# A fifth block product by seven small ones, in a written-out order, in the channel stage of routing attention and an MLP mixer

## The chip, the cores and the metric

The kernel runs on one core of one Trainium2 chip. The metric is the device time of one execution in microseconds (us). All data are float32.

## The reference

Four batches of 768 tokens with 8 heads of 64 go through attention in which a query sees only the keys of its own cluster, and the result, 768 x 512 for each batch, goes through an MLP mixer: a token stage, and a channel stage with 1536 hidden channels.

```python
q_assign = np.argmax(np.einsum('bhsd,hcd->bhsc', q_n, c_n), axis=-1)
k_assign = np.argmax(np.einsum('bhsd,hcd->bhsc', k_n, c_n), axis=-1)
mask = q_assign[:, :, :, None] == k_assign[:, :, None, :]
scores = np.where(mask, scale * np.matmul(q, k.transpose(0, 1, 3, 2)), -1e9)
...                                            # softmax, times v; x is (4, 768, 512)
h = np.maximum(x.transpose(0, 2, 1) @ w_tok1, 0.0) @ w_tok2
u = x + h.transpose(0, 2, 1)
h2 = np.maximum(u @ w_ch1, 0.0) @ w_ch2        # w_ch1 512 x 1536, w_ch2 1536 x 512
return u + h2
```

## The kernel before

The kernel goes through three stages: attention (16 pairs of heads), the token stage (batches 0 and 1, then 2 and 3), and the channel stage, a batch at a time in the order 0, 2, 3, 1. The change lies in the channel stage and the hand-over to it. The order of issue is written out by hand: each engine runs its instructions in the order in which the Python code issues them, and semaphores make an instruction wait for data and for a buffer that is still read.

**A batch and its parts.** The channel stage takes a batch's hidden channels in three parts. A part has a first layer (`ch1_pair`, line 784), which makes hidden blocks, and a second layer (`ch2_chunks`, line 960), which multiplies them by the second weights and adds the result to x. Both layers are written as a 2 x 2 block product with seven products in place of eight (Winograd's form). The seven are in the table `SEVEN` (line 551):

| name | left x right | | name | left x right |
|---|---|---|---|---|
| p1 | A11·B11 | | c12 | S4·B22 |
| p5 | S1·T1 | | c22 | S3·T3 |
| c11 | A12·B21 | | c21 | A22·T4 |
| u2 | S2·T2 | | | |

The S are sums of left blocks (weights in the first layer) and the T are sums of right blocks (the batch's transposed tokens `uT`); `winograd_left` and `winograd_right` yield their four steps each as one VectorE instruction.

**Products of small ones.** In the first part of the first batch (`ch1_plain`) the first layer runs its seven products in two chunks each, and a chunk is 2 matmuls with 384 columns that add up (12 chunks go through `big`, the last two, of c21, come late). In the other 11 parts (`ch1_sets`, line 864) four of the seven are themselves split into 2 x 2 blocks and done by seven small products with 192 columns, with sums of sums: they are called Y (c11), P (p5), Z (c12) and X (c21). `set_lefts` and `set_rights` (lines 602 and 620) name their blocks; `set_left_sums(part)` makes the weights' sums once, in the first batch; `set_right_sums` makes the right sums anew for each batch, into the tile `uTss`. The other three products, p1, u2 and c22, stay big: 2 chunks each, written `big`.

A small product goes to a bank of PSUM (8 banks; tags X, Z with three each and Y with two) and is then added to a block in SBUF by VectorE, at line 566 (`add`), or copied by ScalarE. A second product that accumulates in a bank waits until the first one's addition has read it. In the code, `direct` writes both halves of a bank, `chain` adds up p1, u2, c22 and c21 in one bank with an addition after each, and `column` adds p5 to two blocks.

**What fills the gaps.** `others` is a list of steps on VectorE (sums of weights and operands); `late` is a list with the end of the first layer. `between`, called after each big product of the first layer and after each of the 21 products of the second (`by_turns`, line 746), issues the next of both. `u_steps` turn the next batch's tokens (ScalarE copies and DMA transposes); three of them, `beside`, are issued in the first layer of the batch's last part. `u_sums` yields T1 to T4 of the next batch.

**At a batch's end.** T1 and two sums of P are issued within the last products; then come two sums of Y and Z together and T2, and the rest go to `others`:

```python
yz, x, p = steps
yz[0]()
yz[1]()
next(usums)
others += [lambda: next(usums)] * 2
others.append(lambda: [step() for step in (yz[2], p[2], yz[3], p[3])])
others += [lambda: None, lambda: (x[0](), x[1]()), lambda: (x[2](), x[3]())]
```

Batch 1 is spilled to DRAM after the first half of the token stage and comes back into x0's place when batch 0 is written. Three numbers that say whether this fast path held are counted in the first batch (`fits`, `fits_count`) and read by every engine with `values_load` (`fits_load`, line 1004) ahead of the last second layer; a branch at the end uses them.

Of the kernel before, what the change touches and what calls it, by code (L numbers as in the profile page):

```python
# [50 lines left out]
def kernel(  # L51
# [49 lines left out]
    tokpool = pool("tokpool", 1, tokens)  # L101
    staging = fast.enter_context(ExitStack())
# [30 lines left out]
    spill = spilled.tile([P, NJ, DM], F32, name="spill")  # L133
    xs = [(x1pool if b == 1 else xpool).tile([P, NJ, DM], F32, name=f"x{b}") for b in range(B)]
# [466 lines left out]

    def set_lefts():
        if "l2" not in pools:
            pools["l2"] = pools["w2sums"].tile([P, 4, 3, HS], F32, name="w1ss")
        l2 = pools["l2"]
        yx = W["ch1"].rearrange("p f (i r c) -> p f i r c", i=2, r=2)[:, 2:4]
        pz = pools["w1s"][:, 0:3:2].rearrange("p i f (r c) -> p f i r c", r=2)
        for n, both in enumerate((yx, pz)):
            blocks = [both[:, f, :, r] for r in range(2) for f in range(2)]
            sums_ = [l2[:, 2 * n : 2 * n + 2, m] for m in range(3)]  # L610
            yield dict(
                zip(("A11", "A12", "A21", "A22", "S1", "S2", "S4", "S3"), blocks + sums_ + blocks[2:3])
            )
# [6 lines left out]
    def set_rights():  # L620
        uT, R, r2 = pools["uT"], pools["R"], pools["r2"]
        yz = uT[:, :, 2:4].rearrange("p n f (k t) -> p n f k t", k=2)
        x, p = (R[name].rearrange("p f (k t) -> p f k t", k=2) for name in ("T4", "T1"))
        for blocks, sums_ in (
            ([yz[:, :, f, k] for f in range(2) for k in range(2)], [r2[:, 0:2, m] for m in range(3)]),
            ([x[:, f, k] for f in range(2) for k in range(2)], [r2[:, 2, m] for m in range(3)]),
            ([p[:, f, k] for f in range(2) for k in range(2)], [r2[:, 3, m] for m in range(3)]),
        ):
            yield dict(
                zip(("B11", "B12", "B21", "B22", "T1", "T2", "T4", "T3"), blocks + sums_ + blocks[1:2])  # L630
            )

    def set_right_sums():

        pools["r2"] = pools["w2sums"].tile([P, 4, 3, HS // 2], F32, name="uTss")
        return [list(winograd_right(blocks)) for blocks in set_rights()]

    def set_blocks():

        (yx, pz), (yz, x, p) = (list(y) for y in (set_lefts(), set_rights()))  # L640
        left = {name: {k: a[:, i] for k, a in two.items()} for two, i, name in
                ((yx, 0, "Y"), (yx, 1, "X"), (pz, 0, "P"), (pz, 1, "Z"))}
        right = {"Y": {k: b[:, 0] for k, b in yz.items()}, "Z": {k: b[:, 1] for k, b in yz.items()},
                 "X": x, "P": p}
        return left, right
# [94 lines left out]
    def between(n=1):  # L740
        if late:
            late.pop(0)()
        for _ in range(min(n, len(others))):
            others.pop(0)()

    def by_turns(n, product, of, last=False, after=()):
# [10 lines left out]
        for m in range(len(order) // 2):  # L757
# [9 lines left out]
            between()  # L767
# [16 lines left out]
    def ch1_pair(part, sets, beside):  # L784
# [6 lines left out]
        p5, c12 = (pools["mlp"].tile([P, 2, HS], F32, name=k) for k in ("p5", "c12"))  # L791
# [10 lines left out]

        def big(psum, a, r, i, start):
            product(psum, a, r, i, start)
            between()
            if a != "A11" and beside:
                beside.pop(0)()
# [13 lines left out]
        def sums_34():  # L821
            nc.vector.scalar_tensor_tensor(
                out=h2["S3"], in0=c12, scalar=0.0, in1=a11, op0=ALU.max, op1=ALU.subtract
            )
            sub(h2["S4"], a12, h2["S2"])

        (ch1_sets if sets else ch1_plain)(
            part, product, big, relu, a11, a12, a22, p5, c12, sum_1, sum_2, sums_34
        )

    def ch1_plain(part, product, big, relu, a11, a12, a22, p5, c12, sum_1, sum_2, sums_34):
# [24 lines left out]
        def late_(i):  # L856
            product(X[i], "A22", "T4", i, False)
            nc.scalar.activation(out=a12[:, i], in_=X[i], func=ACT.Relu)
            (sums_34 if i else sum_2)()
# [4 lines left out]
    def ch1_sets(part, product, big, relu, a11, a12, a22, p5, c12, sum_1, sum_2, sums_34):  # L864

        left, right = set_blocks()
        n0, n1 = slice(0, HS // 2), slice(HS // 2, HS)

# [7 lines left out]
        def direct(bank, which, start=True):  # L876
            small(bank[:, n0], which, "c11", start)
            small(bank[:, n1], which, "c12", start)

        def chain(q, which, name, x):  # L880

            small(q[:, n0], which, name, name == "p1")
            src = q[:, n0]
            if len(x.shape) == 3:
                src = src.unsqueeze(1).to_broadcast([P, 2, HS // 2])
            add(x, src, x)

        def column(z, which, x):
            small(z[:, n0], which, "p5")
            add(x[:, :, n1], z[:, n0].unsqueeze(1).to_broadcast([P, 2, HS // 2]), x[:, :, n1])  # L890

        X = [ptile("X", HS), None]
        big(X[0], "A11", "B11", 0, True)
        nc.scalar.copy(out=a11[:, 0], in_=X[0])  # L894
        ybe = ptile("Y", HS)
        direct(ybe, "Y")
        add(a11[:, 0], ybe, a11[:, 0])
        X[1] = ptile("X", HS)
        big(X[1], "A11", "B11", 1, True)
        nc.scalar.copy(out=a11[:, 1], in_=X[1])  # L900
        pbe = ptile("Z", HS)
        direct(pbe, "P")
        nc.scalar.copy(out=p5[:, 0], in_=pbe)
        yq, pq = ptile("Y", HS), ptile("Z", HS)
        chain(yq, "Y", "p1", a11[:, 0, n0])
        chain(pq, "P", "p1", p5[:, 0, n0])
        big(X[0], "S2", "T2", 0, False)
        chain(yq, "Y", "u2", a11[:, 0, n1])
        yz, pz = ptile("X", HS), ptile("Z", HS)
        column(yz, "Y", a11)  # L910
        chain(pq, "P", "u2", p5[:, 0, n1])
        small(pz[:, n0], "P", "p5")
        nc.scalar.copy(out=p5[:, 1, n1], in_=pz[:, n0])
        relu(a11[:, 0])
        add(p5[:, 0, n1], pz[:, n0], p5[:, 0, n1])
        add(c12[:, 0], X[0], p5[:, 0])
        big(X[1], "S2", "T2", 1, False)
        chain(yq, "Y", "c22", a11[:, 1, n1])
        chain(pq, "P", "c22", p5[:, 1, n1])
        direct(ybe, "Z")  # L920
        chain(yq, "Y", "c21", a11[:, 1, n0])
        small(pq[:, n0], "P", "c21", False)
        nc.scalar.copy(out=p5[:, 1, n0], in_=pq[:, n0])
        relu(a11[:, 1])
        add(c12[:, 0], ybe, c12[:, 0])
        chain(yz, "Z", "p1", c12[:, 0, n0])
        add(c12[:, 1], X[1], p5[:, 1])
        big(X[0], "S3", "T3", 0, False)
        add(a22[:, 0], X[0], p5[:, 0])
        relu(a22[:, 0])  # L930
        chain(yz, "Z", "u2", c12[:, 0, n1])
        column(pbe, "Z", c12)
        big(X[1], "S3", "T3", 1, False)
        add(a22[:, 1], X[1], p5[:, 1])
        relu(a22[:, 1])
        chain(yz, "Z", "c22", c12[:, 1, n1])
        direct(X[0], "X", False)
        nc.scalar.copy(out=a12[:, 0], in_=X[0])
        small(X[1][:, n0], "X", "c21", False)
        nc.scalar.copy(out=a12[:, 1], in_=X[1])  # L940
        chain(yz, "Z", "c21", c12[:, 1, n0])
        chain(yq, "X", "p1", a12[:, 0, n0])
        sum_1()

        def late_1():
            chain(yq, "X", "u2", a12[:, 0, n1])
            column(pz, "X", a12)
            sum_2()

        def late_2():  # L950
            chain(yq, "X", "c22", a12[:, 1].rearrange("p (k t) -> p k t", k=2))
            relu(a12)
            sums_34()

        late.extend([late_1, late_2])
# [166 lines left out]
    for b in (0, 2):  # L1122
# [26 lines left out]
        if b == 2:  # L1149
            take(turning, len(turning))  # L1150
            usums = u_sums()
            tok2_chunks(b, {13: lambda: next(usums)})
        else:
# [3 lines left out]
            nc.sync.dma_start(spill, xs[1])  # L1157
# [7 lines left out]
    batches = (0, 2, 3, 1)  # L1165
    for n, b in enumerate(batches):
        turning = []
        for part in range(3):
# [8 lines left out]
            ch1_pair(part, not first, [turning.pop(0) for _ in turning[:UCOLS]])  # L1177
# [5 lines left out]
            if n == 0 and part == 2:  # L1183
                others += set_left_sums(0)
            if last:
                both = fits_load()
            after = {}
# [15 lines left out]
            if part == 2 and not last:  # L1203

                yz, x, p = steps
                yz[0]()
                yz[1]()
                next(usums)

                others += [lambda: next(usums)] * 2  # L1210
                others.append(lambda: [step() for step in (yz[2], p[2], yz[3], p[3])])
                others += [lambda: None, lambda: (x[0](), x[1]()), lambda: (x[2](), x[3]())]
                if n == 0:
                    xs[1] = xpool.tile([P, NJ, DM], F32, name="x0")
                    nc.sync.dma_start(xs[1], spill)
# [182 lines left out]
    with tc.If(both < 3 * P) as fit:  # L1398
# [33 lines left out]
```

## Time and profile before

| | us |
|---|---|
| median of 4 runs (823.25 to 823.74) | 823.34 |
| profiled execution | 823.32 |
| its span | 821.5 |
| TensorE busy | 814.3 |
| VectorE busy | 631.2 |
| ScalarE busy | 374.6 |
| GpSimd busy | 30.6 |

In the profile PE is TensorE, PEld its loading of weights, DVE VectorE, ACT ScalarE, POOL GpSimd and SP the engine that issues most DMAs. Matmuls are shown as pipelined records, so their durations overlap; the distance from one start to the next is the pace. A float32 matmul is two records. Line 798 is the first layer's big product, line 871 the small product, line 966 the second layer's product; lines 563 and 566 are `sub` and `add` on VectorE, line 810 the relu and lines 894 to 940 copies on ScalarE. The channel stage starts at 393.5 us of the span; its parts start at 429.9, 465.4, 500.6, 535.9, 570.9, 605.8, 641.3, 676.2, 711.2, 746.5 and 781.4.

### The profile page before, as it was taken

How to read it: one execution, taken by the hardware profiler on the slowest of the kernel's cores; microseconds unless marked ns; L12 is line 12 of the kernel's file. 1: busy time of each engine (PE TensorE's matmuls, PEld its weight loads, DVE VectorE, ACT ScalarE, POOL GpSimd, SP SyncE). 2: the span in 40 equal slices, each digit the busy share in tenths (PEclk: the TensorE clock that was granted, in tenths of full speed). 3: DMA queues.
4: the chain of work that ended last, by engine and by line, in shares of the span. 5: the costliest groups of instructions: out<-in, count | busy, mean ns of one | idle time of the engine just before them, and what ended most of it. 6: DMA issues, size and time to landing. Idle time of an engine off the chain costs nothing.

```text
span 821.5 us, 11693 instructions
## 1 busy us (share of the span) xinstructions
PE 814.3 (99%) x4348; PEld 535.5 (65%) x4348; DVE 631.2 (77%) x1206; ACT 374.6 (46%) x573; POOL 30.6 (4%) x28
## 2 busy tenths in 40 slices
PE   8999999999999999999999999999999999999997
PEld 4444444444444444444588888888888888888876
DVE  6879898989898978859797788755777566785655
ACT  5588776777878776127202154121441204511120
POOL 1001010111011000000000000000000000000000
PEclk9999999999999999999999999999999999999999
DMA  9797666767676434143000025000140001400002
GB/s 156 132 168 146 134 142 122 149 141 160 131 160 136 98 101 122 51 129 77 0 1 1 4 45 183 1 0 1 38 118 0 1 1 30 125 1 1 1 0 81
DMA packets 184258, 63.41 MB, mean 77 GB/s; under 512 B 172800, under 2 KB 176896, under 8 KB 183936
## 3 DMA queue, kind: packets, MB, share of 16 engines
q1 hardware_dynamic: 182592, 62.18, 34.7%
q8 instruction: 36, 0.59, 0.3%
q10 hardware_dynamic: 1600, 0.39, 0.2%
q14 instruction: 30, 0.25, 0.1%
HBM read 36.21 MB, written 7.86 MB: 54 GB/s over the span
## 4 chain that ended last, share of the span: by engine, by line
PE 98%; DVE 1%; issue 0%; ACT 0%; DVEq 0%; ACTq 0%
PE sc L413 19%; PE av L455 15%; PE pX L966 15%; PE pX L798 12%; PE pZ L966 7%; PE ph L534 5%; PE pY L871 5%; PE pZ L871 4%; PE pX L871 4%; PE pY L966 4%; PE pX L774 3%; PE small L491 2%; PE pZ L774 1%; PE small L304 1%; PE pZ L798 1%; PE pY L774 1%
## 5 line engine op out<-in xcount | busy, mean ns | idle before, releaser
L437 ACT ACTIVATE ex<-sc 128x768 f32<-128x768 f32 x192 | 150.9, 811 | 27.2 <-PE sc L413 15.5
L413 PE MATMUL sc<-qkT 64*128 64x384 f32 x768 | 155.3, 483 | 0.0
L445 DVE TENSOR_TENSOR sum<-sum,ex 128x768 f32<-128x768 f32 x128 | 127.8, 998 | 28.0 <-ACT ex L437 15.8
L455 PE MATMUL av<-ex,va 128*64 128x384 f32 x768 | 127.4, 488 | 0.0
L566 DVE TENSOR_TENSOR x<-pX,x 128x256 f32<-128x256 f32 (+1 forms) x168 | 76.1, 461 | 38.2 <-PE pX L966 37.7
L455 PEld LDWEIGHTS av<-ex,va 128*64 128x64 f32 x768 | 53.7, 137 | 71.7 <-issue 68.0
L413 PEld LDWEIGHTS sc<-qkT 64*128 64x128 f32 x768 | 67.8, 187 | 38.3 <-issue 38.0
L810 ACT ACTIVATE hA<-hA 128x384 f32<-128x384 f32 (+1 forms) x57 | 34.0, 597 | 85.5 <-DVE hA L566 85.5
L566 DVE TENSOR_TENSOR hA<-pY,hA 128x192 f32<-128x192 f32 (+1 forms) x90 | 36.7, 408 | 45.4 <-PE pY L871 42.7
L798 PE MATMUL pX<-uT,wc 128*128 128x384 f32 x192 | 69.8, 487 | 0.0
L894 ACT COPY hA<-pX 128x384 f32<-128x384 f32 x11 | 5.3, 478 | 131.3 <-PE pX L798 131.3
L413 PE MATMUL sc<-ohT 64*128 64x384 bf16 x384 | 62.4, 323 | 0.0
L462 ACT COPY avrows<-av 128x768 uint16<-128x768 uint16 x32 | 25.6, 799 | 43.5 <-PE av L455 43.5
L566 DVE TENSOR_TENSOR x<-pZ,x 128x256 f32<-128x256 f32 (+1 forms) x84 | 36.6, 459 | 11.4 <-PE pZ L966 11.3
L798 PEld LDWEIGHTS pX<-uT,wc 128*128 128x128 f32 x192 | 35.4, 190 | 14.7 <-issue 0.6
L534 PE MATMUL ph<-x,wt 128*128 128x512 f32 x96 | 41.6, 593 | 0.0
L413 PEld LDWEIGHTS <-ohT 64*128 64x128 bf16 x384 | 18.7, 94 | 33.9 <-issue 9.6
L966 PE MATMUL pX<-wc,hA 128*128 128x256 f32 x144 | 36.9, 380 | 0.3 <-ACT hA L940 0.3
L711 ACT COPY uT<-ucols 128x768 uint16<-128x768 uint16 x32 | 33.2, 1051 | 4.8 <-DMA ucols<-urows 4.8
L966 PE MATMUL pZ<-wc,hS 128*128 128x256 f32 x144 | 35.0, 379 | 0.0
L966 PE MATMUL pY<-wc,hA 128*128 128x256 f32 x144 | 35.0, 379 | 0.0
L798 PE MATMUL pX<-uTs,w1s 128*128 128x384 f32 x96 | 34.9, 486 | 0.0
(189 smaller groups left out, 1312.2 us busy)
## 6 DMA issues: line engine op xcount, KB each, us to landing
raw<-in_moe_w_ch_dram SPq DMA_DIRECT2D x24, 512.0 KB, 4.4
va<-in_v_dram SPq DMA_DIRECT2D x16, 384.0 KB, 3.6
out_dram<-x SPq DMA_DIRECT2D x24, 256.0 KB, 2.3
qk<-in_k_dram SPq DMA_DIRECT2D x60, 96.0 KB, 3.8
qk<-in_q_dram SPq DMA_DIRECT2D x60, 96.0 KB, 3.4
raw<-in_moe_w_tok_dram SPq DMA_DIRECT2D x3, 512.0 KB, 4.5
raw<-in_moe_w_tok_dram SPq DMA_DIRECT2D x4, 384.0 KB, 3.8
spill<-x SPq DMA_DIRECT2D x1, 1536.0 KB, 5.1
```

Source lines behind the costliest of these rows:

```text
L413: nc.tensor.matmul(sc[:, h, 0:HS], lhsT=src[rows, 1, j], rhs=src[rows, 0, HJ * qh : HJ * qh + HJ], start=start, stop=not start,)
L437: nc.scalar.activation(out=ex, in_=sc[:, :, 0:HS], func=ACT.Exp, scale=SM_SCALE)
L445: nc.vector.tensor_tensor(out=acc, in0=acc if j > 1 else st["ex", qh, 0], in1=st["ex", qh, j], op=ALU.add)
L455: nc.tensor.matmul(av[h * D : (h + 1) * D], lhsT=st["va"][:, h, j], rhs=ex[:, h], start=(j == 0), stop=(j == NJ - 1),)
L534: nc.tensor.matmul(pf, lhsT=W["tok1"][:, j, t * P : (t + 1) * P], rhs=xs[b][:, j], start=(j == 0), stop=(j == NJ - 1),)
L566: nc.vector.tensor_tensor(out=dst, in0=a, in1=b, op=ALU.add)
L711: nc.scalar.copy(out=out, in_=pools.pop(("ucols", i)).rearrange("p w j t -> p w (j t)"))
L774: nc.tensor.matmul(psum, lhsT=A[a][:, i], rhs=R[r], start=start, stop=True, skip_group_check=not start,)
L798: nc.tensor.matmul(psum, lhsT=A[a][:, k, c], rhs=R[r][:, k], start=start and k == 0, stop=k == 1, skip_group_check=not start,)
L810: nc.scalar.activation(out=x, in_=x, func=ACT.Relu)
L871: nc.tensor.matmul(psum, lhsT=left[which][a][:, part * P : part * P + P], rhs=right[which][r], start=start, stop=True, skip_group_check=no ...
L966: nc.tensor.matmul(psum, lhsT=h2[a][:, k, i * P : (i + 1) * P], rhs=Bw[w][:, part + 3 * k], start=start and k == 0, stop=k == 1, skip_grou ...
```

## The change

S3·T3 (c22) becomes a fifth product done by seven small ones, U. For this there are a block more in `set_lefts` and `set_rights`, a tile `u3` for its result and larger tiles for the sums (5 sets in place of 4). The order of the first layer is written out as a list of names, `CH1`, with a table of banks, `BANKS`. The names read so, with W one of Y, P, Z, X, U: `Wa Wd Wf Wg` are the small products p1, u2, c22 and c21 in one bank, `Wz` is p5, `Wbe` the two direct ones; `+Wa` and so on is the addition on VectorE that reads the bank; `Wc0 Wcz Wcg` are copies on ScalarE. `p1_i` and `u2_i` are the big products' chunks, `a11_i` a copy, `V C B E` additions that put the blocks together, `r11 r22 r12` relus, `s1` to `s4` the second layer's left sums. `yz0` to `u3`, `p2`, `p3`, `T2` to `T4` are the right sums, issued here in the first part of a batch only (`extra`). What stands after the first `|` is issued after the second layer's products, one group each: S1 comes there, after the first product.

The tile of batch 3 gets a place of its own in the token stage and is spilled as well, and both spilled batches come back when two batches before them are written. `between` issues a late step or others, no longer both, and the number of others is chosen so that they last to the end of the second layer; `ch1_sets` issues none. The counts are read after the tenth product of the last second layer.

```diff
-    spill = spilled.tile([P, NJ, DM], F32, name="spill")
-    xs = [(x1pool if b == 1 else xpool).tile([P, NJ, DM], F32, name=f"x{b}") for b in range(B)]
+    spill = {b: spilled.tile([P, NJ, DM], F32, name=f"spill{b}") for b in (1, 3)}
+    homes = (xpool, x1pool, xpool, x3pool)
+    xs = [homes[b].tile([P, NJ, DM], F32, name=f"x{b}") for b in range(B)]
...
-        for n, both in enumerate((yx, pz)):
+        for n, both in ((slice(0, 2), w1[:, 2:4]), (slice(2, 4), pz), (slice(4, 5), w1[:, 0:2, 1:2])):
             blocks = [both[:, f, :, r] for r in range(2) for f in range(2)]
...
+            ([u[:, f, k] for f in range(2) for k in range(2)], [r2[:, 4, m] for m in range(3)]),
...
     def between(n=1):
-        if late:
-            late.pop(0)()
-        for _ in range(min(n, len(others))):
-            others.pop(0)()
+        step = late.pop(0) if late else None
+        if step:
+            step()
+        else:
+            for _ in range(min(n, len(others))):
+                others.pop(0)()
...
-            between()
+            between(-(-len(others) // max(len(order) // 2 - m, 1)))
...
         def big(psum, a, r, i, start):
             product(psum, a, r, i, start)
-            between()
+            between(2 if len(others) <= 12 else 1)
...
+    BANKS = {
+        "Zbe": 0, "Pbe": 0, "Uz": 0, "Ybe": 0, "Yq": 1, "Zq": 2, "X0": 3, "Pq": 4, "Ube": 5, "Pz":
+        5, "Zz": 5, "Yz": 5, "Xz": 5, "Uq": 6, "Xq": 6, "X1": 7,
+    }
+    CH1 = """
+        p1_0 yz0 T2 Zbe a11_0 Ya T3 Zc0 aside Za Pa Pbe +Za +Ya p2 Ube T4 Pc0 u2_0 Uc0 x0 x1 +Pa yz1
+        Pz Pd u0 Pcz Ua p3 Yd yz2 Uz +Pz Zd u1 Ucz Zz +Pd p1_1 yz3 Zcz +Ua u2 +Zz Pf +Yd +Zd a11_1
+        aside Ud u3 Yf +Uz Yz +Ud Ybe +Yf V0 Zf +Pf Uf +Ybe Yg +Yz Pg u2_1 x2 x3 Pcg +Zf r11_0 +Yg
+        +Uf r11_1 C0 Zg Ug Zcg Ucg B0 r22_0 Xbe V1 C1 Xa E0 B1 r22_1 aside +Xa
+        |
+        s1
+        |
+        Xz Xd Xg +Xd E1 +Xz
+        |
+        Xf +Xf r12 s2
+        |
+
+        |
+
+        |
+        s4
+        |
+
+        |
+        s3
+    """
...
+        bank = [ptile(tag, HS) for tag in "XXXZZZYY"]
+        X = [bank[BANKS["X0"]], bank[BANKS["X1"]]]
+        target = {"Y": a11, "P": p5, "U": u3, "Z": c12, "X": a12}
...
+            do[f"V{i}"] = lambda: add(a22[:, i], X[i], p5[:, i])
+            do[f"C{i}"] = lambda: grow(c12[:, i], a22[:, i])
+            do[f"B{i}"] = lambda: grow(a22[:, i], u3[:, i])
+            do[f"E{i}"] = lambda: add(a12[:, i], X[i], u3[:, i])
...
+            nc.sync.dma_start(spill[3], xs[3])
...
             if last:
-                both = fits_load()
-            after = {}
+                after[9] = lambda: loaded.append(fits_load())
...
-                if n == 0:
-                    xs[1] = xpool.tile([P, NJ, DM], F32, name="x0")
-                    nc.sync.dma_start(xs[1], spill)
+                for name, sums_ in zip(("yz", "x", "p", "u"), steps):
+                    for m, step in enumerate(sums_):
+                        if name != "p" or m > 1:
+                            extra[f"{name}{m}"] = step
+                for m in (2, 3, 4):
+                    extra[f"T{m}"] = lambda: next(usums)
+                if n < 2:
+
+                    later = batches[n + 2]
+                    xs[later] = xpool.tile([P, NJ, DM], F32, name=f"x{b}")
+                    nc.sync.dma_start(xs[later], spill[later])
```

## The prediction

> **What bounds the kernel now.** I read the page first (busy times, then the chain), then the chain in order of time, then each engine's instructions around the start of one batch.
>
> ```profile
> PE 814.3 (99%) x4348; PEld 535.5 (65%) x4348; DVE 631.2 (77%) x1206; ACT 374.6 (46%) x573; POOL 30.6 (4%) x28
> PE 98%; DVE 1%; issue 0%; ACT 0%; DVEq 0%; ACTq 0%
> ```
>
> TensorE is busy for 99% of the span and is 98% of the chain, at a granted clock of 1.00 throughout. So a column that TensorE need not stream is time that goes, unless VectorE, next at 77%, makes TensorE wait. The chain in order of time (start, length, what) gives TensorE's pace:
>
> ```profile
> 570.86 1.29 PE pX L798 x4
> ...
> 584.77 1.62 PE pX L871 x10
> ...
> 603.24 2.59 PE pX L966 x12
> 605.83 1.29 PE pX L798 x4
> ...
> 620.86 0.04 issue
> 620.90 0.92 PE pX L871 x4
> ...
> 797.31 0.34 issue
> 797.64 1.10 PE pX L966 x4
> ```
>
> Every float32 matmul is two records. Records of 384 columns come every 0.3235 us (1.29 for 4), of 192 every 0.1618 (1.62 for 10), of 256 every 0.216 (2.59 for 12). A part of the channel stage has 24, 56 and 84 of them: 7.76 + 9.06 + 18.14 = 34.97. The part that starts at 570.86 ends at 605.83, in 34.97: TensorE never waits in it. The next, a batch's first part, ends at 641.25 and takes 35.42; of the 0.45 that it loses, the rows at 620 show 0.04 + 0.27 (0.92 for 0.65 of matmuls). The rows at 797 are the read of the counts: 0.34 idle and 1.10 for 0.86 of matmuls, 0.58 in all. VectorE in that first part, by start and duration:
>
> ```profile
> 610.40 0.35 DVE L566 TENSOR_TENSOR hA<-pY,hA 128x192 f32<-128x192 f32 x1
> 610.67 0.35 DVE L566 TENSOR_TENSOR p<-pZ,p 128x192 f32<-128x192 f32 x1
> 610.93 0.55 DVE L563 TENSOR_TENSOR uT<-uT 128x384 f32<-128x384 f32 x1
> 611.40 0.36 DVE L563 TENSOR_TENSOR uTs<-uTs 128x192 f32<-128x192 f32 x1
> ```
>
> Durations are 0.35 (192 columns) and 0.55 (384), but the next instruction starts after 0.27 and 0.47; with 768 columns (duration 0.95) after 0.87, with 256 (0.42) after 0.34. One that needs the instruction just ahead starts 0.03 to 0.10 after its end.
>
> **The change part by part.**
>
> (1) *The fifth product.* In each of the 11 parts that use small products (all but the first), S3·T3 goes from 8 records of 384 (2.588 us) to 14 of 192 (2.265). That is 0.3235 off the path, 11 times: **-3.56**.
>
> (2) *What VectorE pays in every part.* Now 14 additions of 192, 10 of 384, 4 of 768 and 21 of 256: 3.7 + 4.7 + 3.5 + 7.0 = 18.9 us start to start. After: 18 of 192 and 12 of 384, so 20.9 of the 34.64 that TensorE will need. VectorE stays ahead, so only the order can make TensorE wait. I walked it with the trace's delays: TensorE to VectorE or ScalarE 0.20 (issue ends 605.66, addition starts 605.86; 606.95, copy at 607.15), VectorE back to TensorE 0.05 (addition ends 620.85, matmul 620.90). The thinnest places are two ScalarE copies ahead of a bank's reuse: "Ucg" is done 0.08 before "Xa" is due, "Zc0" 0.24 before "Pbe". ScalarE has 16 instructions in place of 12 in these parts, some 7 us of 34.64. Cost 0; were each part 0.1 late here it would be about +1.
>
> (3) *A batch's first part (3 times).* T2, T3, T4 (0.87 each), the four joint Y/Z sums (0.47) and ten of x, p and U (0.27) now lie between the products: 2.6 + 1.9 + 2.7 = 7.1. With 17 x 0.27 + 9 x 0.47 = 8.7 of additions that is 15.9, and 16.4 with dependences, beside TensorE's 15.2 up to "Xa". VectorE is full, so I walked both engines from the first matmul at 0. VectorE ends the last batch at 0.55 and starts yz0 0.55, T2 1.02, T3 1.89, +Za 2.79, +Ya, p2, T4 3.59, x0, x1, +Pa 5.22, yz1 5.49, u0, p3, yz2 6.49, +Pz 6.96, and so on to +Zz 8.76, +Uz 9.8, +Zf 13.1, +Uf 13.7, +Xa 16.9, +Xd 18.8. Against TensorE, "due" being without any wait: "Ube" needs T3: due 3.56, it ends 2.84. "Pd" writes the bank that +Pa reads: due 5.82, free 5.62. "Zz" 7.44 and 7.36. "Ybe" 10.35 and 10.22. "Zg" 13.59 and 13.53. "Ug" 13.91 and 14.07: late by 0.16. "Xf", then due at 18.93, finds its bank read by +Xd until 19.2: late by 0.27. So 0.43 is lost where 0.31, 0.45 and 0.31 were before (parts of 35.28, 35.42 and 35.28 against 34.97): **+0.22** for the three. Bounds: -1.07 if all these waits go; four margins lie under 0.15, and 0.6 more in each batch makes +2.0.
>
> The Trainium skill speaks against this step ("VectorE: DVE Perf Modes", section "The DRAIN you can't avoid"): there the next VectorE operation does not start until the pipe has emptied, and the count of operations is what should be kept low. Rows of this trace start 0.27 apart where one lasts 0.35, so the pace here is not the duration; a walk by the rule would come to rival A.
>
> (4) *The first batch's weights' sums.* U's blocks add four instructions to each of three sets; with 128 columns I take 0.20 start to start (0.27 less 64 columns at about 1 ns). In the first part 18 steps ride on 12 big products, one or two each, where VectorE now idles 0.3 to 1.3 us ahead of most additions: 0. In the second part 20 steps lie in the second layer's turns alone; VectorE ends some 2 us behind, but the next part first writes the banks concerned 1.3 to 2.3 us in, just after they are free. The one wait there now, 0.31 ahead of "c22" (due 457.84, starts 458.15), comes to 0.14: **-0.17**, from -0.31 to +0.5.
>
> (5) *The second spill.* x3 is written out (1.5 MB; 5.1 us to landing in x1's row) once its last addition ends near 392, so by 399; SP issues nothing else between 385 and 469. The tile over it, the weights' second sums, is first written near 402. The load back follows the second batch's outputs as x1's follows the first's, and is used 65 us later. Cost 0; uncovered, VectorE waits 3 us where TensorE has several products of slack: +0.5.
>
> (6) *The counts' read* moves from the start of the last second layer to its tenth product. TensorE pays 0.58 now, where the matmuls just ahead had only just been let go. At the tenth product all operands are long there, so I take half: **-0.28**, from -0.58 to +0.2. VectorE and ScalarE have slack there, and SP has nothing to issue yet.
>
> (7) *S1 and the later steps.* S1 now comes after the second layer's first addition. On the clock of (3) it ends at 18.6 and is needed at 19.2; S2 ends at 21.9, for 23.9; the last relu at 22.0, for 22.1. Nothing beyond (3).
>
> Sum: 823.32 (the profiled execution: span 821.5 and 1.8 around it; the median is 823.34) - 3.56 + 0.22 - 0.17 - 0.28 = **819.5**. A measurement of this kernel can tell about 0.2% (1.65 us) from no change.
>
> **Rivals.**
>
> *A: VectorE becomes the bound at the batches' starts* (slower). Should an instruction hold VectorE for its duration, those up to +Xa take 17 x 0.355 + 9 x 0.55 + 8.6 (10 x 0.355 + 4 x 0.55 + 3 x 0.95) = 19.6 instead of 15.9, and "Xd" and "Xf" come 3.3 late, not 0.43: three times 2.9 is +8.6. The first batch's second part would hold 24 us of VectorE work beside 18.1 of matmuls and add 1 at least: 819.5 + 9.6 = 829. It turns the sign early: the sum's 3.8 us are 1.27 in each of three batches, or 0.03 on each of 43 instructions, a third of the way from 0.27 to 0.355. For it: the walk has no slack left. Against: the start-to-start rows, from the same mix of operations.
>
> *B: no waits are left.* The order spreads the sums, and (3), (4) and (6) come out at their best: 823.32 - 3.56 - 1.07 - 0.31 - 0.58 = 817.8; midway to the forecast, 818.6. For it: the thin places of the walk are all under 0.3.
>
> *C: bank reuse eats the gain.* Five products share one bank and four another. Should each of the 11 parts lose 0.2 to 0.3, as "pX" at 620.90 does now, 2.2 to 3.3 come back: 822.2. For it: the margins 0.08 and 0.24 of every part. Against: the part from 570.86 has such reuse too, and no wait.
>
> That the fifth product does not shorten TensorE's work at all would need small records slower than 0.185 (2.588 / 14); ten in a row run at 0.162.
>
> **How the numbers follow.** Forecast (818.9 to 820.6) 0.58; B 0.12; C and other ways to no change (821.7 to 825.0) 0.12; between forecast and C 0.08; A or another loss 0.10. Faster by over 0.2% (below 821.7): 0.58 + 0.12 + 0.08 = 0.78; same 0.12; slower 0.10. The range 818.0 to 822.2 leaves out A, C above its middle and B's lower end, 0.2 in all.
>
> **What would show it.** TensorE: 4348 + 11 x 6 = 4414 records, 34.64 for a steady part (1). VectorE: some 1300 instructions, 668 us busy (2). A batch's first part 34.9 to 35.2, with TensorE waiting for VectorE late in the first layer (3). Wrong: such parts of 36 or more (A); 34.9 in all eleven (C); a gap of TensorE near 400 (the spill); 0.5 or more idle near the tenth product of the last layer (6).

## The result and the profile after

The changed kernel takes **821.92 us** (median of 40 runs, 821.24 to 822.75); the kernel before took 823.21 beside it (60 runs, 822.4 to 824.1). The ratio is **0.9984**, with a 95% interval of 0.9980 to 0.9988: 1.3 us faster, a third of the 3.8 forecast. That is a little under the 0.2% named there as what can be told from no change, but over this many runs the interval leaves no change out. The profiled execution took 821.96, with a span of 820.2 (before 823.32 and 821.5).

The page's busy times and chain of the changed kernel:

```profile
PE 812.7 (99%) x4414; PEld 542.7 (66%) x4414; DVE 654.6 (80%) x1300; ACT 390.5 (48%) x617; POOL 30.7 (4%) x28
PE 94%; DVE 5%; issue 1%; ACT 0%; DVEq 0%; ACTq 0%
```

The counts are those of the sum: 66 matmul records more, 94 VectorE instructions more. TensorE, though, is now 94% of the chain, not 98%, and VectorE 5%, not 1%: some 40 us of the chain now run through VectorE. The chain in order of time (start, length, what), at the starts of parts:

```profile
571.33 1.29 PE pZ L804 x4
...
603.43 2.59 PE pX L1001 x12
606.02 1.29 PE pZ L804 x4
...
641.44 1.29 PE pZ L804 x4
```

The steady part from 571.33 now takes 606.02 - 571.33 = 34.69, where it took 34.97. The batch's first part behind it takes 641.44 - 606.02 = 35.42, just as before: there the whole gain is gone.

For a balance I took each matmul record's start less the start of the record ahead of it less that one's pace (0.0008427 us a column); what remains is a wait of TensorE. From the start of the channel stage to the end these waits sum to 2.4 us before and to 4.65 after:

| place (time after) | before | after |
|---|---|---|
| first batch, part 2: copy of c12's bank (433.2) | 0 | 0.65 |
| first batch, part 2: c22 in the second layer (458.7) | 0.41 | 0.80 |
| three first parts of a batch, together | 1.10 | 2.2 |
| Xf in two other parts (485.1, 660.2) | 0 | 0.44 |
| Xa in the eight other parts | 0 | 0.24 |
| read of the counts | 0.58 | 0 |
| counts' own three-column matmuls, and one of 0.04 | 0.3 | 0.3 |

The fifth product's -3.56 and the waits' +2.23 make -1.33, and the span went from 821.5 to 820.2. So TensorE's work shrank as computed, and waits took 2.2 of 3.6 us back. The experiments below take these waits away one by one; the theory was that each is a separate matter of order or of a shared buffer, the rival that VectorE's added work must be paid for somewhere. All are measured beside the kernel before in the same way; times to compare with 821.9.

### The profile page after: what moved, and what is told of

It reads as the page before. It is cut to its first block, busy times and chain, and to the rows that moved or that the text cites. A ratio compares the mean times of both kernels' runs of the same rounds, so it can differ in the third digit from the quotient of the medians.

```text
span 820.2 us, 11990 instructions
## 1 busy us (share of the span) xinstructions
PE 812.7 (99%) x4414; PEld 542.7 (66%) x4414; DVE 654.6 (80%) x1300; ACT 390.5 (48%) x617; POOL 30.7 (4%) x28
## 4 chain that ended last, share of the span: by engine, by line
PE 94%; DVE 5%; issue 1%; ACT 0%; DVEq 0%; ACTq 0%
PE sc L415 19%; PE av L457 15%; PE pX L1001 13%; PE pZ L1001 7%; PE pX L924 6%; PE ph L536 5%; PE pZ L924 5%; PE pZ L804 4%; PE pY L1001 4%; PE pY L804 3%; PE pY L924 3%; PE pX L780 3%; PE small L493 2%; DVE hA L568 1%; PE pX L804 1%; PE pZ L780 1%
## 5 line engine op out<-in xcount | busy, mean ns | idle before, releaser
L966 ACT COPY hA<-pZ 128x384 f32<-128x384 f32 x11 | 5.3, 480 | 128.5 <-PE pZ L804 128.5
L1001 PE MATMUL pX<-wc,hA 128*128 128x256 f32 x144 | 35.0, 379 | 0.0
L1001 PE MATMUL pX<-wc,hS 128*128 128x256 f32 x144 | 33.4, 380 | 0.4 <-DVE x L568 0.4
L536 PEld LDWEIGHTS ph<-x,wt 128*128 128x128 f32 x96 | 18.2, 190 | 23.1 <-issue 22.6
L1001 PE MATMUL pX<-w2s,hA 128*128 128x256 f32 x144 | 33.2, 379 | 0.0
L1001 PE MATMUL pZ<-w2s,hS 128*128 128x256 f32 x144 | 33.0, 379 | 0.0
```

Source lines behind the costliest of these rows:

```text
L536: nc.tensor.matmul(pf, lhsT=W["tok1"][:, j, t * P : (t + 1) * P], rhs=xs[b][:, j], start=(j == 0), stop=(j == NJ - 1),)
L1001: nc.tensor.matmul(psum, lhsT=h2[a][:, k, i * P : (i + 1) * P], rhs=Bw[w][:, part + 3 * k], start=start and k == 0, stop=k == 1, skip_grou ...
```

## The experiments

**The test's numbers in a buffer of their own.** The chain of the changed kernel at the first of these waits:

```profile
431.90 0.35 DVE good L1032
...
432.37 0.18 DVE good L1032
...
432.63 0.49 ACT c L952
...
433.16 0.92 PE pX L924 x4
```

The row of ScalarE in its timeline, with the idle time ahead and its releaser in brackets:

```profile
432.63 0.48 ACT L952 COPY c<-pX 128x384 f32<-128x384 f32 x1 [0.91 <-DVE good L1032]
```

The copy Zc0, from the bank that X's products want next, writes c12. The test (`fits`) that VectorE runs at the end of the part keeps its numbers in a tile with the tag "c12", the same buffer, so the copy waits 0.91 for the test's last reduction. Before, c12 was first written in this part long after the test's last reduction, by VectorE itself (timeline of the kernel before):

```profile
431.62 0.17 DVE L997 TENSOR_REDUCE good<-inside 128x1 f32<-128x16 f32 x1
...
437.90 0.56 DVE L566 TENSOR_TENSOR c<-pX,p 128x384 f32<-128x384 f32 x1
```

```diff
-        inside = pools["mlp"].tile([...], F32, tag="c12", name="inside")
+        inside = pools["mlp"].tile([...], F32, tag="inside", name="inside")
```

> Theory: the fifth product gave its whole 3.56 us, and TensorE's waits in the channel stage rose from 2.42 to 4.65 us. One of them, 0.65 at 433.15, is there because the tile of the counts' test shares the buffer of c12, which ScalarE now writes as the first copy of a part. With a tile of its own the copy waits only for its matmul: that wait goes, about -0.65 against the changed kernel, so 1.3 + 0.65 = 1.9 to 2.0 us below the kernel before. Rival: VectorE is behind there anyway (its last additions end 1.3 us into the part), so the wait only moves on to the next use of a bank: less than 0.2 is gained, 1.3 to 1.5 us below the kernel before.

821.40, ratio 0.9976 (0.9967 to 0.9985), span 819.3. The copy, in the timeline of this run:

```profile
431.83 0.48 ACT L952 COPY c<-pX 128x384 f32<-128x384 f32 x1
```

It starts 0.8 earlier, nothing ahead of it, and the wait of 0.65 is gone; the other waits are what they were, within 0.03 each. So this wait goes when the buffer is no longer shared. Two things had moved in the changed kernel to make it: the copy came 6 us earlier, and the test itself ended 0.75 later (its last reduction ends at 432.54 after, at 431.79 before). With the test at its old time the copy, due at 431.83, would hardly have waited; no run moves the test alone.

**The counts' read back at the start of the last second layer.**

```diff
-                after[9] = lambda: loaded.append(fits_load())
+                loaded.append(fits_load())
```

> Undoes one move alone: the counts are read ahead of the last second layer again. Theory: the read then stalls TensorE for 0.5 to 0.6 us, where it stalls nothing after the tenth product (VectorE's 1.00 us idle there is hidden): 0.5 to 0.6 us more than the changed kernel, 0.7 to 0.8 below the kernel before, and the profile shows 0.5 us between the last small product and the first of the second layer. Rival: it is the order of the small products around it that let the 0.58 go, and the read is hidden in both places: no change, 1.3 below the kernel before.

822.70, ratio 0.9997 (0.9988 to 1.0006), span 820.9. The first matmul of the last second layer, in this run's timeline:

```profile
796.72 1.97 PE L1001 MATMUL pX<-wc,hA 128*128 128x256 f32 x8 [0.78 <-PE pY L924]
```

It is 1.02 late in all; before it was 0.58. Read at the tenth product, the same costs TensorE nothing; only VectorE idles there, in the timeline of the changed kernel:

```profile
807.81 0.42 DVE L568 TENSOR_TENSOR x<-pX,x 128x256 f32<-128x256 f32 x1 [1.00 <-PE pX L1001]
```

So the move is worth 0.58 against before, and more in the new order.

**Two of the right sums earlier.** In a batch's first part, T2 and T3 are made in the batch before it.

```diff
+                after[16] = lambda: next(usums)
+                after[18] = lambda: next(usums)
-                for m in (2, 3, 4):
+                for m in (4,):
```

> T2 and T3 of the next batch are issued within the last products of the second layer (after the 17th and the 19th), where VectorE has 0.5 us free beside each product, and no longer in a batch's first part. Theory: that part loses time because VectorE's 16 us are beside 15 us of matmuls; with 1.73 us less of it the waits of 0.36 at the small products go in all three, and most of the 0.37 at Xf: 1.1 to 2.1 us less than the changed kernel, 2.4 to 3.4 below the kernel before. Rival: what counts is the latency of each addition, copy and matmul in its bank's chain, not the amount: less than 0.3 is gained, or the sums delay the last additions of the second layer and a new wait of 0.3 to 0.5 comes at Zbe or Ya in each.

821.67, ratio 0.998 (0.9971 to 0.9989): no gain beyond what the runs scatter, and the waits of the three first parts are unchanged (only Xf's 0.22 at 660, in another part, is gone). With 1.74 us less work at the start, VectorE only waited (its timeline):

```profile
502.90 0.55 DVE L565 TENSOR_TENSOR uTss<-uT 128x384 f32<-128x384 f32 x1
504.21 0.36 DVE L568 TENSOR_TENSOR c<-pX,c 128x192 f32<-128x192 f32 x1 [0.76 <-PE pX L924]
```

The second row is +Za, which cannot start before TensorE's product Za. All waits of the first part come later, at Zz, Ug and Xf, and what was queued behind +Za was the same as ever. Less work ahead of +Za saves nothing there; its theory, that the amount of work in the part counts, failed. The next run asks whether the place counts. The wait at Ug, in the timeline of the changed kernel:

```profile
514.83 0.35 DVE L568 TENSOR_TENSOR u<-pY,u 128x192 f32<-128x192 f32 x1
...
515.24 0.59 PE L924 MATMUL pY<-uTss,wc 128*128 128x192 f32 x2
```

The first row is +Uf, which ends at 515.18; Ug, in the same bank, was due at 515.14 and starts at 515.24.

**Less work behind +Za.** The same, and the idle time filled: T4 and two more steps go ahead of +Za.

```diff
-        p1_0 yz0 T2 Zbe a11_0 Ya T3 Zc0 aside Za Pa Pbe +Za +Ya p2 Ube T4 Pc0 u2_0 Uc0 x0 x1 +Pa yz1
+        p1_0 yz0 T4 Zbe a11_0 Ya p2 yz1 Zc0 aside Za Pa Pbe +Za +Ya Ube Pc0 u2_0 Uc0 x0 x1 +Pa
```

> Against the changed kernel (821.9 us): in a batch's first part T4, the second sum of P and the second pair of sums of Y and Z are done before +Za, in the 0.76 us that the last run left idle there, so 1.6 us less VectorE work lies behind +Za. Theory (what is queued on VectorE behind +Za makes Zz, Ug and Xa late): the waits near 509 and 515 us (0.36 in each of three first parts) go, and with them -0.7 to -1.2 us in all; the wait at Xf (0.37 each) stays or shrinks a little. Rival (each wait is the latency of one chain of addition and sum, whatever lies before): under 0.3 us in all.

820.63, ratio 0.997 (0.9959 to 0.9982), span 818.7. Of the 0.73 in each first part 0.35 went, all of Zz, Zg and Ug; Xf's 0.37 stayed to the hundredth (the 0.22 at 660 is gone here too). The waits sum to 3.39. The rival, a latency that no queue changes, is out for Zz and Ug, but stands for Xf.

**Xf one product later.** The timeline of the changed kernel around that wait:

```profile
518.22 0.35 DVE L568 TENSOR_TENSOR hA<-pY,hA 128x192 f32<-128x192 f32 x1
...
518.49 0.42 DVE L568 TENSOR_TENSOR x<-pX,x 128x256 f32<-128x256 f32 x1
...
518.89 0.96 DVE L824 SCALAR_TENSOR_TENSOR hS<-c,hA 128x768 f32<-128x768 f32 x1
...
519.06 0.49 PE L924 MATMUL pY<-uTss,wc 128*128 128x192 f32 x2
...
519.77 0.42 DVE L568 TENSOR_TENSOR x<-pX,x 128x256 f32<-128x256 f32 x1
520.11 0.35 DVE L568 TENSOR_TENSOR hA<-pY,hA 128x192 f32<-128x192 f32 x1
...
520.51 0.59 PE L924 MATMUL pY<-uTs,wc 128*128 128x192 f32 x2
```

On VectorE these are +Xa, an addition of the second layer, S1, a second addition and +Xd; Xf is the matmul at 520.51, which wants the bank that +Xd reads. Xd's own product ends by 519.06 (the row there is Xg), but S1 and the second addition stand ahead of +Xd. Two runs moved Xf back by one product of the second layer. The first:

```diff
+        
+        |
         Xf +Xf r12 s2
-        |
-        
         |
```

> Theory: Xf finds its bank still read by +Xd in five parts (0.37 three times, 0.21, 0.23, in all 1.55 us), since VectorE takes s1 first. Issued one product later it is due 0.86 us later and waits nowhere. The relu ahead of c11 may come 0.1 to 0.2 late in the three first parts. So 1.0 to 1.5 us less than the changed kernel, 2.3 to 2.8 below the kernel before. Rival: the amount of VectorE's work is the bound, not the place of Xf; then the same lag shows at c11 or at c22, and less than 0.3 is gained.

860.01, ratio 1.0447 (1.0432 to 1.0461). The page's group of c11's matmuls in the second layer (busy, mean | idle ahead):

```profile
L1001 PE MATMUL pY<-wc,hA 128*128 128x256 f32 x144 | 41.2, 428 | 31.5 <-ACT hA L820 31.5
```

Of the 38 us, TensorE waits 31.5 for the relu r12, some 10 in each of three batches. About 7 more are a slower TensorE behind these three waits, as in the chain of this run behind the first of them:

```profile
499.64 2.13 PE pY L1001 x5
...
506.83 2.59 PE pX L1001 x12
```

The first row has 0.43 from record to record, the second the usual 0.216. The slow stretches last 5.2, 3.4 and 6.4 us, at a granted clock of 0.50 to 0.53, where the stretch from 506 to 510 us has 1.00; no wait of 1.3 us or less is followed by one. As for the waits themselves: at this point the turning of the next batch's tokens, copies on ScalarE that wait for transposing DMAs, is issued too, and the relu had come to stand behind it. An edit to one engine's order had changed another's. The second moved the turning along:

```diff
-                after[3] = lambda: take(turning, len(turning))
+                after[4] = lambda: take(turning, len(turning))
```

> Against the changed kernel (821.9 us): Xf with its addition, relu and S2 comes one product later, and the turning of the next batch one step later too, so that ScalarE's order is the same as before. Theory (Xf is held by VectorE, which runs S1 and an addition ahead of +Xd, which frees the bank): the waits at Xf go, 0.37 in each of three first parts, 0.21 and 0.23 in two others, so -1.0 to -1.5 us. Rival (the relu behind Xf is then late for c11): as much comes back as a wait of c11 in each of eleven parts, 0 to +1 us.

823.61, ratio 1.0004 (0.9995 to 1.0013). The 10 us are gone and so are the waits at Xf, but the chain shows what took their place:

```profile
523.35 0.85 ACT hA L820
...
524.25 1.99 PE pY L1001 x8
```

The relu (0.85) behind +Xf is now late for c11, by 0.51 in each of three first parts, by 1.33 and 0.68 in the first batch's other two, and by 0.07 in the remaining six: 4.0 lost for the 1.55 of Xf and the 0.8 of c22 saved. That is the rival's case, with more coming back than it allowed.

**S1 behind +Xd.**

```diff
-        s1
+        none
         |
-        Xz Xd Xg +Xd E1 +Xz
+        Xz Xd Xg +Xd s1 E1 +Xz
```

> Against the changed kernel (821.9 us): S1 is issued behind +Xd instead of ahead of it, nothing else. Theory (Xf waits only because S1 and an addition of the second layer stand ahead of +Xd on VectorE): +Xd then starts near 519.3 instead of 520.1 us on the first part's clock, Xf is due at 520.2, and all the waits at Xf go: 3 x 0.37 + 0.23 + 0.21 = -1.5 us, so 820.4. S1 would end near 520.4 and the second layer's p5 is due near 520.6, so 0.1 may come back per part. Rival (VectorE's work has to be done before p5 in any case, so the wait moves from Xf to p5): -0.3 to +1 us.

823.09, ratio 1.0 (0.9991 to 1.0009). Again Xf waits nowhere and again it comes back, 0.21 in each of 11 parts: 0.07 at p5, which needs S1, and 0.14 at c11, whose operand is now made later. That is 2.3 lost for 1.55 saved, and c22's wait in the first batch grew by 0.3.

**Eight sums of weights in the first layer, then four.** The chain of the changed kernel at the wait of c22:

```profile
457.11 0.34 DVE x L568
457.45 0.86 DVE hS L832
458.31 0.35 DVE x L568
...
458.70 3.00 PE pX L1001 x12
```

S3 (0.86) comes between two additions, and the second frees c22's bank; VectorE is behind with the weights' sums put between them. The first try gave eight of them to the places where later batches make their right sums, which are empty in this part:

```diff
+            if n == 0 and part == 1:
+                lefts = list(left_sums(2)) + list(set_left_sums(2))
+                for name in "yz0 T2 T3 p2 T4 x0 x1 yz1".split():
+                    extra[name] = lefts.pop(0)
...
```

> Against the changed kernel (821.9 us): in the second part of the first batch eight of the twenty steps of weights' sums are done in the first layer. Theory (VectorE is behind in the second layer, so c22's bank is freed and S3 is done late at 458.7 us, and Xf waits in the part behind it): the wait of 0.8 us near 458.7 goes, -0.5 to -0.8 us, perhaps 0.2 more near 485. Rival (S3's own chain of dependences holds c22, or the first layer waits instead): under 0.2 us, or slower by up to 0.5.

822.0, ratio 0.9986 (0.9977 to 0.9995). The wait of c22 is gone and one of 0.97 has come at 436.9. The chain there:

```profile
435.82 0.42 DVE w1ss L565
436.24 0.34 DVE wc L565
436.58 0.28 DVE p L568
...
436.90 0.59 PE pZ L924 x2
```

Sums of weights (w1ss, wc) stand ahead of the addition to p that frees the bank. The second try gives only four, where the trace of the changed kernel has VectorE idle for 0.86 us or more:

```diff
+                lefts = list(left_sums(2))
+                for name in "x0 u0 p3 u2".split():
+                    extra[name] = lefts.pop(0)
...
```

> Against the changed kernel (821.9 us): of the twenty steps of weights' sums in the first batch's second part, four (0.6 us each) are issued in the first layer, each in a place where VectorE idles 0.9 us or more. Theory (VectorE's backlog in the second layer holds c22, and the run that moved eight only lost it again because it put them where VectorE had no time): the wait of 0.8 us near 458.7 goes and none comes near 437, -0.5 to -0.8 us, so 821.1 to 821.4. Rival (any sum in the first layer delays a small product): the wait near 437 stays at 0.4 or more, under 0.3 us in all.

821.21, ratio 0.9977 (0.9968 to 0.9987), span 819.1. The chain where c22 waited:

```profile
456.51 1.73 PE pZ L1001 x8
458.24 1.94 PE pX L1001 x9
```

No wait there, none at 437.

**All together, three times.** First a kernel with the edits for the buffer, the queue behind +Za, Xf and the turning one product later, eight sums in the first layer (in the places "yz0 T4 p2 yz1 x0 x1 u0 p3"), and:

```diff
-        +Uf ... C1 Xa E0 B1 r22_1 aside +Xa
+        +Uf ... C1 Xz Xa E0 B1 r22_1 aside +Xa
...
-        Xz Xd Xg +Xd E1 +Xz
+        Xd Xg +Xd E1 +Xz
```

> The changed kernel with the test's numbers in a buffer of their own, less VectorE work behind +Za, Xf and the turning one step later, eight sums of weights in the first layer, and Xz ahead of Xa. Theory (the gain of the fifth product went into waits that its order makes, each of them separate): 0.65 + 0.5 to 0.8 + 0.7 to 1.2 + 1.0 to 1.5 and 0.3 from Xa go, so 821.9 - 3.2 to 4.4 = 817.5 to 818.8 us, faster than both kernels. Rival (VectorE's work is what is paid for, so waits come back at other places): 820 to 821.5 us.

821.79, ratio 0.9985 (0.9976 to 0.9994): its two bad parts brought their own waits, 1.28 at 436.6 and c11's everywhere. Then with the four sums in place of the eight, and Xf and the turning back where they were, but S1 behind +Xd:

```diff
-        s1
+        none
         |
-        Xz Xd Xg +Xd E1 +Xz
+        Xd Xg +Xd s1 E1 +Xz
```

> The changed kernel with the test's numbers in a buffer of their own (0.65), less VectorE work behind +Za (1.2), S1 behind +Xd (1.5 less what the shorter queue has taken already, 1.1 to 1.5), four sums in idle places (0.5 to 0.8) and Xz ahead of Xa (0.03 in each of 11 parts). Theory (the gain of the fifth product was spent on separate waits of its order): 821.9 - 3.5 to 4.4 = 817.5 to 818.4 us, faster than both kernels, with only the three-column matmuls near 466 us left of the waits. Rival (VectorE's work must be paid for somewhere): 819.5 to 820.5 us.

819.78, ratio 0.9963 (0.9949 to 0.9977). Waits of 2.7, of which S1's 0.21 in each part are 2.3. Last, with S1 in its old place, and only the second layer's second addition moved behind +Xd and the E1 and +Xz that follow it:

```diff
             x = of(to, i)
+            if m == 1 and late:
+                between()
+                add(x, banks[tag, i], x)
+                continue
             add(x, banks[tag, i], x)
```

> The kernel of the last run with S1 back ahead of +Xd, and only the second layer's second addition (0.34) moved from ahead of +Xd to behind it; the second weights' sums in idle places, the test's own buffer, the shorter queue behind +Za and Xz ahead of Xa are kept. Theory (S1 behind +Xd cost 0.2 in each of eleven parts as waits of p5 and c11; what must leave +Xd's way is 0.13 us, and the addition is enough): +Xd starts near 519.8 and ends 520.1 on the first part's clock, Xf is due at 520.2, and neither Xf nor p5 nor c11 waits; of 2.7 us of waits some 0.3 to 0.8 stay, so 819.8 - 1.9 to 2.4 = 817.4 to 817.9 us. Rival (any order gives VectorE's work back as waits): Xf or c11 late by 0.1 to 0.2 in each part, 819 to 820 us.

**818.31**, ratio **0.9937** (0.9924 to 0.9951), span 816.3: faster than both kernels. Page and chain:

```profile
PE 810.1 (99%) x4414; PEld 542.9 (67%) x4414; DVE 653.9 (80%) x1300; ACT 390.4 (48%) x617; POOL 30.7 (4%) x28
...
PE 99%; DVE 0%; ACT 0%; issue 0%; DVEq 0%
```

```profile
638.53 1.29 PE pZ L808 x4
...
673.20 1.29 PE pZ L808 x4
...
707.86 1.29 PE pZ L808 x4
...
742.75 1.29 PE pZ L808 x4
```

VectorE does the same 1300 instructions in the same busy time, and yet the chain is TensorE's again. Steady parts take 34.67 and the first part of a batch 34.89; the waits sum to 1.0, 2.4 in the kernel before: 0.3 at the counts' matmuls and 0.2 in each first part are most of it. The rival, that VectorE's added work must be paid for, is refuted: in this order it is not, so nearly all of the waits were the order's. Of the edits in it, Xz ahead of Xa was not run alone.

## Why the prediction was right and wrong

The direction was right and the time lies inside the range, but the gain was forecast three times too large. TensorE's work shrank as forecast; the steps that failed are (3), the waits at a batch's start, and (4), the wait in the first batch's second part. By its steps:

- **(1) the fifth product** held: -3.56 is what the balance needs, and a steady part went from 34.97 to 34.69 (forecast 34.64).
- **(2) VectorE in every part** nearly held. The margin of 0.08 at "Ucg" was not there: Xa is 0.03 late in each part; the 0.24 at "Zc0" was. VectorE's busy time grew by 23.4, not by the 37 of "What would show it": the durations of its records do sum to 36.2 more, but the page counts the time once where two records overlap, and the overlaps grew by 12.8. Two of the printed sums are slightly low, without weight here: the counts in (2) give 19.1 and 21.1 for 18.9 and 20.9, and the additions in (3) 8.8 for 8.7.
- **(3) the batch's first part** failed in size: +1.1 instead of +0.22. The walk had Ug late by 0.16 and Xf by 0.27; the trace has Zg and Ug late by 0.12 and Xf by 0.26. What it put at nothing is the price behind these waits: the second record of the delayed matmul comes late too, by 0.10 at Ug and 0.11 at Xf, and by 0.11 at Zz, whose margin of 0.08 was no margin. With Xa's 0.03 that makes 0.73 for 0.43. The rows of before held it already: what the rows at 620 show there is 0.21 of wait and 0.11 at the next record. And the walk counted VectorE's work from the start of the part; the runs show that less of it ahead of +Za saves nothing, and less of it behind +Za does.
- **(4) the first batch's sums** failed in sign: +1.04 instead of -0.17. The shared buffer of the test was overlooked (0.65): the step looked at banks and at VectorE's time, and c12's first writer had moved from 437.9 to 431.8, with the test's end 0.75 later. And c22's wait grew from 0.41 to 0.80 instead of shrinking, because S3 itself, with sums ahead of it, came late; with four of the sums moved to idle places that wait was gone.
- **(5) the spill** held: no gap of TensorE near 400 beside the 0.04 of before.
- **(6) the counts' read** was better than forecast: -0.58, the end of its range, since TensorE waits for nothing there.
- **(7) S1 and the later steps** was off by 0.44: Xf waits in two other parts too (0.21 and 0.23), for the same order of S1, addition and +Xd.

Together -3.56 + 0.24 + 1.1 + 1.04 - 0.58 + 0.44 = -1.3, as measured. Rival C has the time nearest to this (822.2), but not by its mechanism: it gave 0.2 to 0.3 to each of the 11 parts, where 0.03 was lost. Rival A's mechanism did not show: rows 518.22 and 518.49 above start 0.27 apart where one lasts 0.35. The rule weighed in (3), of the Trainium skill ("VectorE: DVE Perf Modes", "The DRAIN you can't avoid"), would have put 2.9 more on each first part; the section's own note that an instruction which is not held starts earlier, which the prediction left out, is what agrees with these rows. (The advice on the count of operations stands on the same page, under "Rules for kernel authors".) Rival B's end, 817.8 to 818.6, is what the last experiment reaches (818.31), with a better order than the change had.

## What to carry to other kernels

When a change takes work off an engine that is busy for 99% of the time, add up the engine's work and its waits apart: here the work came off to the hundredth, and a net two thirds of it went into waits, which had five causes. Look for every buffer whose first writer moves to an earlier time or whose last reader moves to a later one, test tiles and scratch with a borrowed tag among them, and ask which instruction stands directly ahead of the one that frees a bank. What decided here was not how much the second engine had to do, but what was queued between the last point where it had to wait and the next point where it was waited for. And a step moved to save a wait in five parts can cost one in eleven.

## What the hardware showed that was not expected

A semaphore wait could cost TensorE more than its delay. A pair of records of 192 columns lasts 0.49 in the timeline (0.16 apart); a delayed pair lasts 0.59, as at 520.51 above, so its second record is 0.10 to 0.11 late as well. In the channel stage of both kernels it was so for every wait of the layers' matmuls of 0.09 or more (0.08 behind the read of the counts), and for some whose first record was hardly delayed, as here (timeline of the changed kernel; six records from 612.34 at 0.162 end at 613.31):

```profile
612.34 1.14 PE L924 MATMUL pX<-uTss,w1ss 128*128 128x192 f32 x6
613.33 0.59 PE L924 MATMUL pZ<-uTss,w1ss 128*128 128x192 f32 x2
```

At Xa the second record alone is late, by 0.03. Why the second record is late, and at which short waits, the runs do not show.

And a read of three numbers into all engines' registers costs TensorE 0.58, 1.02 or nothing, by where it is issued: 1.02 just behind the first layer's last matmuls in the new order, nothing after the tenth product of the second layer.
